# A long convolution's inverse transform: operands of its first stage exchanged, its last stage with a small table and wide products

## The chip, the cores and the metric

The kernel runs on one core of one Trainium2 chip. The time is the device time of one execution in microseconds. The core's engines work side by side: PE (matrix products; PEld is its loading of the stationary operand), ACT and DVE (elementwise work, both may read PSUM, where the PE writes), POOL (elementwise work on SBUF alone), and SP, which here only issues DMAs. SBUF and PSUM have 128 partitions. All data is 32-bit.

## The reference

One transformer-like block for 2048 tokens of 640 channels: a modulated layer norm, a gated long convolution (H3), and a modulated MLP with squared ReLU.

```python
kv_f = rfft(pad(conv4(k, shift_k) * v, S)); kf_f = rfft(pad(ssm_k, S))
y = irfft(kv_f * kf_f)[:S] + kv * ssm_D
x = q + ga * (h1(q) * y)                   # h1, h2: layer norms, scaled and shifted
out = x + gb * (relu(h2(x) @ w1 + b1) ** 2 @ w2 + b2)
```

The modulation rows (`ga`, `gb` and so on) come from `silu(c) @ w_mod`. The convolution runs per channel with transforms of length 4096.

## The kernel before, in words

**Convolution.** The 640 channels are taken as five blocks `b` of 128. A transform of 4096 is written as matrix products in two steps. A token is 64 n + i, with n from 0 to 31 and i from 0 to 63. `unit_a` (L374) contracts n with the table `cw`: four 64*64 tiles of the PE array per group of channels, copied by ACT from PSUM to `AX`. `spectrum` (L395) contracts i with twiddle tables `gb`, once for the kernel `h` and once for the data `x`; `front` (L421) multiplies the two spectra on DVE and adds on POOL, which gives `w` (in parts of `WE` and `WX`), with frequencies on partitions and 128 channels free.

**Inverse.** `back` (L449) does the first stage: the table `gi` is stationary, the products `w` move, and the result has (real or imaginary, i) on 128 partitions; ACT copies it into `QT`, per group of four channels (32 residues m, 4 channels). `unit_t` (L537) transposes four such groups on the PE and ACT copies them to `TS`, two buffers in `WX2`. `unit_y` (L548) does the last stage for one `unit_t`: the transposed data is stationary, the table `ca` (256 columns) moves, 64 columns at a time; 16 matmuls per unit, eight units per block, so 128 a block. Two units share a PSUM tile with the tag Y (two buffers). The result has token mod 128 on partitions and goes to `UP` (16 rows of 128 tokens, 128 channels) by ACT for blocks 0 to 2, by DVE for block 3; for block 4 DVE multiplies it right there with the gate. In block 4 `unit_t2` (L525) transposes half tiles instead, and the last product is cut in two (`y_rest`, L575).

**Around it.** `kv_k`, `kv_s`, `kv_v`, `kv_m` (L232 to L284) make the convolution's input for a later block: PE transposes of k (`kt`, in PSUM under tags X, T or Y), an ACT copy, three DVE passes, a DVE product with v, and a store to `kv_d`, from where `load_x` fetches it. `stats1` (L299) takes mean and variance of q's rows (`q_big`, `q_load`, L926 to L934, load them); `load_xp` (L485) loads q's columns of one block; `prep_a`, `prep_m`, `prep_p` and `gate` normalise, scale and gate; `finish_near` and `finish_add` add q. The parts of the first 256 tokens stay in SBUF, the others go through `x1_d`.

**Order.** The order on each engine is the order in which the program is written: for each block ten steps FS(b, j) (`front` and `back`) and 18 steps GS(b, s), eleven for the last block. `UNITS` (L1111) gives, by block, the steps s at which the next block's `unit_a` (first list), the `unit_t` (second) and the `unit_y` (third) are issued; `at(...)` places everything else, before or after the `unit_a` of a step (`AFTER`). In one step `unit_y` comes first, then `unit_t`. `keep_order` holds the engines to it. All loads and most stores are issued on SP, in order; `sp_dma` lets an issue wait until the one four before it has landed.

**MLP.** After the last block, eight chunks of 256 tokens go through the two products (`mlp_front` L723, `mlp_back` L805) and out by `mlp_out` (L840).

Of the kernel before, what the change touches and what calls it, by code (L numbers as in the profile page):

```python
# [11 lines left out]
F32 = mybir.dt.float32  # L12
# [6 lines left out]
P = 128  # L19
# [12 lines left out]
def _constants():  # L32
# [35 lines left out]
    ca = np.zeros((32, 2, 2, 2, 2, 2, 16, 2))  # L68
    t2 = np.arange(16)
    for h in range(2):  # L70
        nn = 2 * t2 + h
        th = 2 * np.pi * ((m[:, None] * nn[None, :]) % 64) / 64
        a, b = 2 * np.cos(th) / N, -2 * np.sin(th) / N
        a[0] = 1.0 / N
        b[0] = (-1.0) ** nn / N
        for g in range(2):
            for d in range(2):
                ca[:, g, d, 0, h, g, :, d] = a
                ca[:, g, d, 1, h, g, :, d] = b
# [6 lines left out]
        "ca": ca.reshape(128, 256).astype(f),  # L86
# [6 lines left out]
def ssm_mlp_kernel(  # L93
# [70 lines left out]
    TS = [WX[2][:, 4 * j : 4 * j + 4] for j in range(2)]  # L164
# [7 lines left out]
    ca = WX[1][:, 8:10].rearrange("p r (h n) -> p r h n", h=2)  # L172
# [26 lines left out]
    xsrc = kv_d.rearrange("(g a) (n i) -> (a n) g i", a=4, i=64)  # L199
    pt = {}  # L200
# [173 lines left out]
    def unit_a(b, i, q):  # L374
# [74 lines left out]
    def back(b, j):  # L449
        if j == 0:  # L450
            QT[b] = sb.tile([P, DG, 32, 4], F32, tag="S4", name=f"q_{b}")
# [7 lines left out]
        for u in range(4):  # L459
            w = ws[b, 2 * j + u // 2]  # L460
            for r in range(2):
                for a in range(2):
                    l = slice(64 * a, 64 * a + 64)
                    pe.matmul(  # L464
                        t[a][:, u],
                        gi[l, 4 * j + u, r],
                        w[r][l, u % 2],
# [3 lines left out]
        m = 8 * j  # L471
        for g in (slice(0, 16), slice(16, 32)) if end else (slice(0, 32),):
            for a in range(2):
                copy(
                    dve if a and end else act,
                    QT[b][:, g, m + a : m + 8 : 2, :],
                    t[a].rearrange("p m (g d) -> p g m d", d=4)[:, g],
                )
# [6 lines left out]
    def load_xp(b):  # L485
        t = sb.tile([P, NL, P], F32, tag=f"XP{b % 2}", name=f"xp_{b}")
        src = q[:, b * P : (b + 1) * P].rearrange("(l p) d -> p l d", p=P)
        for l in range(0, NL, 4):
            sp_dma(t[:, l : l + 4], src[:, l : l + 4])
        XPt[b] = t  # L490
# [31 lines left out]
    ys, tss = {}, {}  # L522


    def unit_t2(b, g):  # L525
# [788 lines left out]
```

## Time and profile before

| | |
|---|---|
| three runs | 693.88, 696.73, 690.06 us (median 693.88) |
| the profiled execution | span 692.6 us from the first to the last instruction; the page gives no time around it |
| mean granted clock of the PE | 0.990 |
| PE busy | 656.1 us (95%), 8741 matmul records, 8741 weight loads |
| DVE, ACT, POOL busy | 414.1, 326.1, 255.2 us |
| last stage `y` on the PE | 45.1 us, 1280 records |
| first inverse stage `qp` | 42.4 us, 640 records |
| transposes `t` | 22.5 us, 192 records |
| MLP | from 293.2 us to the end |

A page of the profile lists busy time per engine, then groups of instructions by line and operand names (output <- inputs), and the chain of waits that ended last. Names of tiles stand without their numbers. A busy PE isn't a PE at its peak: matmuls are pipelined and their ends are modelled. "Idle before" names what ended an engine's wait; "issue" there means that nothing in the profile explains it.

### The profile page before, as it was taken

What the parts mean: (1) busy time and instruction counts of PE and PEld (TensorE: products, weight loads), DVE (VectorE), ACT (ScalarE), POOL (GpSimd) and SP (SyncE); (2) the same over time, 40 slices, a digit from 0 to 9 for tenths busy, and PEclk for the clock granted to TensorE, in tenths of its full rate; (3) what the DMA queues carried; (4) which work ended last, traced back from release to release, by engine and by line L of the source; (5) the groups of instructions that cost most, each with busy time, mean ns of one, the idle gap of its engine ahead of it and who ended that gap; (6) DMA issues with size and microseconds to landing.
All of it is one profiled execution on the core that took longest, in us unless ns stands there. A gap on an engine that the chain in (4) does not pass through costs nothing.

```text
span 692.6 us, 20344 instructions
## 1 busy us (share of the span) xinstructions
PE 656.1 (95%) x8741; PEld 608.5 (88%) x8741; DVE 414.1 (60%) x783; ACT 326.1 (47%) x688; POOL 255.2 (37%) x299
## 2 busy tenths in 40 slices
PE   6699789898999998999999999999999999999996
PEld 5689678797898897899999999999999999999996
DVE  4257656677787587668665564555645555555633
ACT  4426556767985995547424323333233233233221
POOL 1053155548978879553500301402203204003301
PEclk9999999999999999999999999999999999999999
DMA  9996889878772463456120020010010200200001
GB/s 235 256 255 188 226 240 271 238 209 206 198 237 65 136 185 106 134 145 210 26 77 0 1 77 1 7 71 1 38 39 1 76 2 1 77 1 0 39 1 39
DMA packets 110958, 74.72 MB, mean 108 GB/s; under 512 B 48658, under 2 KB 96146, under 8 KB 110868
## 3 DMA queue, kind: packets, MB, share of 16 engines
q1 hardware_dynamic: 108912, 72.87, 37.2%
q8 instruction: 69, 1.13, 0.7%
q10 hardware_dynamic: 1892, 0.54, 0.3%
q14 instruction: 21, 0.17, 0.1%
q0 software_dynamic: 64, 0.01, 0.0%
HBM read 58.98 MB, written 14.42 MB: 106 GB/s over the span
## 4 chain that ended last, share of the span: by engine, by line
PE 83%; DMA 5%; DVE 4%; ACT 4%; issue 2%; POOL 1%; SPq 0%; POOLq 0%; DVEq 0%; ACTq 0%
PE acc L823 27%; PE h L735 23%; PE pa L383 5%; PE qp L464 5%; PE x L398 4%; PE y L555 4%; PE h L398 3%; PE h L748 2%; PE t L544 2%; PE h L739 1%; DMA p<-kv_d 1%; PE xtp L700 1%; PE vt L276 1%; PE kt L239 1%; ACT q L146 1%
## 5 line engine op out<-in xcount | busy, mean ns | idle before, releaser
L823 PE MATMUL acc<-w_S,hring 128*128 128x320 f32 x960 | 156.7, 311 | 0.2 <-DVE hring L157 0.2
L735 PE MATMUL h<-xt,w_S 128*128 128x512 f32 (+1 forms) x770 | 149.6, 340 | 0.0
L823 PEld LDWEIGHTS acc<-w_S,hring 128*128 128x128 f32 x960 | 144.8, 188 | 4.8 <-DVE hring L157 0.7
L735 PEld LDWEIGHTS h<-xt,w_S 128*128 128x128 f32 x770 | 120.1, 189 | 14.1
L157 DVE TENSOR_TENSOR hring<-mtmp,hring 128x256 fp32r<-128x256 f32 x112 | 67.4, 601 | 69.9 <-ACT hring L146 69.9
L157 POOL TENSOR_TENSOR xt<-we,xt 128x256 fp32r<-128x256 f32 x35 | 27.5, 785 | 201.2 <-ACT xt L146 201.2
L154 DVE TENSOR_TENSOR mtmp<-h,mtmp 128x256 f32<-128x256 f32 (+1 forms) x99 | 41.9, 423 | 96.5 <-ACT mtmp L780 94.0
L780 ACT ACTIVATE mtmp<-h,b1t 128x256 f32<-128x256 f32 x91 | 43.2, 475 | 113.9 <-PE h L735 113.9
L146 ACT ACTIVATE hring<-mtmp 128x256 fp32r<-128x256 f32 x112 | 46.1, 411 | 73.9 <-DVE mtmp L782 63.2
L383 PE MATMUL pa<-wx,p 64*64 64x64 f32 x2560 | 49.4, 230 | 14.0 <-issue 7.9
L383 PEld LDWEIGHTS pa<-wx,p 64*64 64x64 f32 x2560 | 44.2, 143 | 19.9 <-issue 14.2
L146 ACT ACTIVATE a<-pa 128x512 f32<-128x512 f32 x80 | 43.1, 607 | 21.9 <-PE pa L383 21.7
L151 DVE TENSOR_TENSOR wx<-x,wx 128x512 f32<-128x512 f32 x64 | 40.8, 682 | 17.1 <-PE x L398 10.2
L555 PE MATMUL y<-wx,wx 128*64 128x64 f32 x1280 | 45.1, 225 | 4.1 <-ACT wx L146 2.5
L555 PEld LDWEIGHTS y<-wx,wx 128*64 128x64 f32 x1280 | 40.3, 138 | 8.9 <-ACT wx L146 4.0
L398 PE MATMUL x<-a,gb 128*64 128x128 f32 x640 | 42.7, 279 | 3.1 <-DVE wx L151 1.8
L782 DVE SCALAR_TENSOR_TENSOR mtmp<-mtmp 128x256 f32<-128x256 f32 x91 | 39.6, 435 | 3.1
L398 PEld LDWEIGHTS x<-a,gb 128*64 128x64 f32 x640 | 37.0, 140 | 4.5 <-PE h L398 2.5
L261 DVE SCALAR_TENSOR_TENSOR KV<-kt,tap,KV 128x511 f32<-128x511 f32 (+2 forms) x48 | 35.9, 748 | 7.5 <-ACT ktail L146 5.9
L154 POOL TENSOR_TENSOR wm<-wm,wm 128x640 f32<-128x640 f32 x20 | 32.1, 1604 | 15.9 <-ACT wm L341 15.5
L146 ACT ACTIVATE q<-qp 128x512 f32<-128x512 f32 (+1 forms) x40 | 21.3, 584 | 34.5 <-PE qp L464 34.3
L146 ACT ACTIVATE xt<-we 128x256 fp32r<-128x256 f32 x37 | 15.3, 415 | 43.4 <-DVE we L705 43.4
(152 smaller groups left out, 1117.8 us busy)
## 6 DMA issues: line engine op xcount, KB each, us to landing
wm<-in_w_mod_dram SPq DMA_DIRECT2D x25, 320.0 KB, 4.2
KV<-in_A_k_dram SPq DMA_DIRECT2D x20, 256.0 KB, 4.3
KV<-in_A_v_dram SPq DMA_DIRECT2D x20, 256.0 KB, 4.5
p<-in_A_ssm_k_dram SPq DMA_DIRECT2D x20, 256.0 KB, 4.9
p<-kv_d SPq DMA_DIRECT2D x20, 256.0 KB, 4.6
xp<-in_A_q_dram SPq DMA_DIRECT2D x20, 256.0 KB, 4.3
q<-in_A_q_dram SPq DMA_DIRECT2D x15, 320.0 KB, 5.0
out_dram<-x SPq DMA_DIRECT2D x14, 320.0 KB, 2.1
```

Of the source, the lines that this page charges most:

```text
L146: act.activation(o, i, AF.Copy)
L151: eng.tensor_mul(o, a, b)
L154: eng.tensor_add(o, a, b)
L157: eng.tensor_sub(o, a, b)
L261: dve.scalar_tensor_tensor(o, tk[:, : 512 - t], tap[:, b, t : t + 1], o, op0=ALU.mult, op1=ALU.add)
L383: pe.matmul(t[e][64 * r : 64 * r + 64, g].rearrange("p m d -> p (m d)"), pt[b][l, i, 8 * q + g, :], cw[l, r], start=True, stop=True,)
L398: pe.matmul(t[64 * a : 64 * a + 64, s + r], gb[:, g, r, a], AX[b][i][:, 2 * g + a], start=True, stop=True,)
L555: pe.matmul(y[64 * h : 64 * h + 64, 4 * (g % 2) + i].rearrange("p c l d -> p (c l d)"), tss[g][:, i, 64 * r : 64 * r + 64], ca[:, r, h], s ...
L735: pe.matmul(*x, start=(b == 0 and x is both), stop=(b == NB - 1 and x is both))
L780: act.activation(r, h[:, 1], AF.Identity, bias=b1t[:, f : f + 1])
L782: dve.scalar_tensor_tensor(r, r, 0.0, r, op0=ALU.max, op1=ALU.mult)
L823: pe.matmul(acc[2 * s + i], h[:, a, s * P : (s + 1) * P], w[:, y, i * 320 : (i + 1) * 320], start=(f == 0 and ti == 0), stop=(f == NF - 1 ...
```

## The change

In `back` the two operands are exchanged: the products `w` are stationary, the table `gi` moves, and channels come out on partitions. `QT` becomes [128 channels, 64 values of i, 64 of (m, real or imaginary)]. `unit_t` transposes two values of i at a time for all 128 channels, in every block; in block 4 the copies alternate between ACT and DVE. `TS` has six buffers, in `WX2`, `WX1` and `WX3`. `unit_y` takes four `unit_t` at once: the table, now 64 rows (twice) by 32 columns, is stationary, and 512 columns (four pairs, 128 channels) move; eight matmuls of eight different 64*32 tiles, into two PSUM tiles with tag Y; two units per block. A token is now 64 n + 16 c + l, with partition 32 c + n, so a partition holds 16 tokens in a row (l), and the loads of q and the stores of the output go by c, 32 partitions at a time. `unit_a` writes `AX` with the channels in their own order. The first unit of block 4 gives l from 0 to 7, so its statistics (`finish_near(4, 0)`, `stats2(0)`) are placed at GS(4, 4) and GS(4, 5), ahead of the second unit, and `y_rest` and `unit_t2` are gone.

```diff
     def unit_a(b, i, q):
...
-            c = 64 * e + 16 * q
-            o = AX[b][i][:, :, c : c + 16].rearrange("p m (g d) -> p m g d", d=2)
-            copy(act, o, t[e].rearrange("p g m d -> p m g d"))
+            o = AX[b][i][:, :, 32 * q : 32 * q + 32].rearrange("p m (g e d) -> p m g e d", e=2, d=2)
+            copy(act, o[:, :, :, e], t[e].rearrange("p g m d -> p m g d"))
...
     def back(b, j):
...
                     pe.matmul(
                         t[a][:, u],
+                        w[r][l, u % 2],
                         gi[l, 4 * j + u, r],
-                        w[r][l, u % 2],
...
+        for a in range(2):
+            c = 16 * j + 8 * a
+            copy(
+                dve if a and end else act,
+                QT[b][:, :, c : c + 8],
+                t[a].rearrange("p u (r n) -> p n (u r)", r=2),
+            )
...
     def load_xp(b):
...
-        for l in range(0, NL, 4):
-            sp_dma(t[:, l : l + 4], src[:, l : l + 4])
+        for a in range(4):
+            sp_dma(t[32 * a : 32 * a + 32], qsrc[a, :, :, b * P : (b + 1) * P])
...
     def unit_t(b, g):
         t = ps.tile([P, 4, P], F32, tag="T", name=f"t_{b}_{g}", bufs=2)
+        n = 16 * (g % 4) + 8 * (g // 4)
         for i in range(4):
-            pe.transpose(t[:, i], QT[b][:, 4 * g + i].rearrange("p m d -> p (m d)"), ident)
-        tss[g] = TS[g % 2]
-        copy(act, tss[g], t)
+            x = QT[b][:, n + 2 * i : n + 2 * i + 2].rearrange("p n k -> p (n k)")
+            pe.transpose(t[:, i], x, ident)
+        tss[g] = TS[g % 6]
+        copy(dve if b == NB - 1 and g % 2 else act, tss[g], t)

     def unit_y(b, g):
...
+        y = [ps.tile([P, 4, P], F32, tag="Y", name=f"y_{b}_{g}_{i}", bufs=2) for i in range(2)]
+        for a in range(4):
+            for i in range(2):
+                l = slice(64 * i, 64 * i + 64)
+                pe.matmul(
+                    y[i][32 * a : 32 * a + 32].rearrange("p l d -> p (l d)"),
+                    ca[l],
+                    tss[4 * g + a][l].rearrange("p i d -> p (i d)"),
+                    start=True,
+                    stop=True,
+                )
+        for i in range(2):
+            uo = UPt[b][:, 8 * g : 8 * g + 8].rearrange("p (l i) d -> p i l d", i=2)[:, i]
             if b < NB - 1:
-                copy(act if b < 3 else dve, uo, y)
+                copy(act if b < 3 else dve, uo, y[i])
             else:
...
+                dve.tensor_mul(uo, y[i], uo)
...
     def mlp_out(n):
...
             if n < NC - 1:
                 add(dve if s else pool, X1t[n][:, s], t, X1t[n][:, s])
-                sp_dma(out[l * P : (l + 1) * P, :], X1t[n][:, s])
                 continue
             for i in range(2):
...
-                (act.dma_start if i else sp_dma)(out[l * P : (l + 1) * P, o], X1t[n][:, s, o])
+                if s or i:
+                    o = o if s else slice(0, D)
+                    for a in range(4):
+                        (act.dma_start if a % 2 else sp_dma)(
+                            osrc[a, :, 2 * n + s, o], X1t[n][32 * a : 32 * a + 32, s, o]
+                        )
+        if n < NC - 1:
+            for a in range(4):
+                sp_dma(osrc[a, :, 2 * n : 2 * n + 2], X1t[n][32 * a : 32 * a + 32])
...
     def q_load(t, l0, n):
+        for a in range(4):
+            sp_dma(t[32 * a : 32 * a + 32, 0:n], qsrc[a, :, l0 : l0 + n])
         for i in range(n):
-            sp_dma(t[:, i], q[(l0 + i) * P : (l0 + i + 1) * P, :])
             qt[l0 + i] = t[:, i]
...
-        ([0, 1, 4, 11, 13, 16, 16], [1, 3, 3, 5, 5, 6, 7, 9], [3, 4, 4, 6, 7, 8, 8, 11]),
-        ([2, 2, 5, 5, 10, 10, 12], [1, 4, 4, 7, 8, 11, 13, 14], [4, 7, 7, 11, 13, 13, 16, 17]),
-        ([1, 2, 5, 7, 8, 11, 14], [1, 2, 5, 7, 9, 11, 13, 15], [4, 7, 8, 9, 13, 14, 16, 17]),
-        ([0, 3, 4, 6, 9, 11, 14], [1, 2, 4, 7, 8, 11, 14, 14], [4, 6, 8, 10, 11, 14, 17, 17]),
-        ([], [1, 1, 2, 2, 5, 5, 6, 6], [4, 5, 5, 6, 6, 8, 9, 9]),
+        ([0, 1, 4, 11, 13, 16, 16], [1, 3, 3, 5, 5, 6, 7, 9], [6, 11]),
+        ([2, 2, 5, 5, 10, 10, 12], [1, 4, 4, 7, 8, 11, 13, 14], [9, 16]),
+        ([1, 2, 5, 7, 8, 11, 14], [1, 2, 5, 7, 9, 11, 13, 15], [9, 17]),
+        ([0, 3, 4, 6, 9, 11, 14], [1, 2, 4, 7, 8, 11, 14, 14], [9, 17]),
+        ([], [1, 1, 1, 2, 2, 3, 3, 4], [3, 6]),
```

More of the change, by code (lines that the diff above doesn't have):

```diff
@@ L1144, in ssm_mlp_kernel @@
         for s in range(11 if last else 18):
[L1145 removed]
+            if s == sy[0] and not last:
                 u_tile(b)
[L1147 removed]
+            for g in range(2):
                 if sy[g] == s:
```

94 lines of the change are left out of this document (17 added, 77 removed).

## The prediction

> **What bounds the kernel now.** I read the table of stages first: the span cut where one block of 128 channels passes from its spectral half to the half that holds the inverse's last steps. "GS" below is that second half. A row gives the stretch, its length, and each engine's busy time (with instructions), then clock, DMA share and rate.
>
> ```profile
> core 0: us, PE busy (x) PEld busy (x) DVE busy (x) ACT busy (x) POOL busy (x), PEclk, DMA share, GB/s
> 60.00:91.00 31.00, 24.50 (x712) 21.99 (x710) 19.68 (x42) 17.72 (x34) 3.91 (x12) 1.00 0.78 218
> 91.00:117.00 26.00, 25.46 (x463) 23.89 (x462) 18.15 (x32) 14.48 (x27) 16.27 (x25) 1.00 0.94 263
> 117.00:147.40 30.40, 27.75 (x776) 24.34 (x778) 19.57 (x40) 23.17 (x44) 13.15 (x18) 0.94 0.81 223
> 173.40:201.50 28.10, 26.91 (x844) 24.24 (x843) 21.62 (x31) 26.77 (x57) 22.98 (x25) 1.00 0.71 201
> 226.30:249.60 23.30, 22.41 (x752) 20.14 (x752) 14.18 (x18) 22.64 (x50) 18.33 (x13) 1.00 0.59 150
> 275.30:293.20 17.90, 17.41 (x350) 14.91 (x351) 11.79 (x26) 8.98 (x20) 10.33 (x12) 1.00 0.47 138
> 293.20:692.60 399.40, 393.77 (x2569) 370.63 (x2567) 220.46 (x461) 138.90 (x313) 88.20 (x85) 1.00 0.12 40
> ```
>
> The MLP, 399.4 us, has the PE busy for 393.8; the change touches only its stores. The rows of GS(0) to GS(3) differ: in GS(0) the PE idles 6.5 us, beside DMA at 0.78 and more; in GS(1) it has 27.75 of 30.4; in GS(2) and GS(3) the ACT is as full as the PE (26.77 of 28.1, 22.64 of 23.3). The part that changes most is `y`; the same table for its instructions alone shows what there is to win:
>
> ```profile
> 117.00:147.40 30.40, 8.48 (x256) 7.88 (x256) 0.00 (x0) 1.87 (x3) 0.94 0.81 223
> 173.40:201.50 28.10, 8.78 (x256) 7.95 (x256) 0.00 (x0) 1.98 (x3) 1.00 0.71 201
> ```
>
> **The last stage on the PE.** The timeline gives start, length and form (rows*columns of the stationary tile, then the moving operand):
>
> ```profile
> 49.03 2.06 PE L464 MATMUL qp<-wx,gi 64*128 64x128 f32 x32
> ...
> 61.69 1.16 PE L383 MATMUL pa<-wx,p 64*64 64x64 f32 x64
> 62.78 1.15 PE L555 MATMUL y<-wx,wx 128*64 128x64 f32 x32
> ```
>
> Each matmul leaves two records. `pa` uses four 64*64 tiles of the array, `y` two of 128*64: 64 records by four and 32 by two are both 16 rounds, and both take 1.09 us to the next start. So tiles run side by side, and a round of 64 columns costs 68 ns. `qp`, 16 rounds of 128 columns in 1.99 us, gives 124 ns, so each further column costs 0.88 ns and a round of 512 about 462 ns. The new unit has 16 records on eight 64*32 tiles: two rounds, **0.93 us**, against 4 x 1.09 = 4.34 us for the four units it replaces. No row shows 64*32. The bounds are one tile at a time, 16 rounds or 7.4 us, and eight; I take eight, since two and four both paid in full. At four it would be 1.85, at two 3.7. A block falls from 8.7 to 1.9 us: 6.8 us off the PE. The first inverse stage keeps its 16 matmuls of 128 columns per call, so I price the exchange of operands at zero; both waited for the POOL's product anyway.
>
> **What takes the gain's place.** In GS(2) the ACT decides:
>
> ```profile
> 186.53 0.64 ACT L146 ACTIVATE up<-y 128x512 f32<-128x512 f32 x1 [0.80 <-POOL xp L154]
> ...
> 201.77 0.64 ACT L146 ACTIVATE up<-y 128x512 f32<-128x512 f32 x1 [0.21 <-PE y L555]
> 202.64 0.60 ACT L146 ACTIVATE wx<-h 128x512 f32<-128x512 f32 x1 [0.24 <-PE h L398]
> ```
>
> These are most of its gaps in 28 us. The ACT keeps 16 forward copies, 8 transposed copies and 4 output copies per block. By form they read:
>
> ```profile
> L146 ACT ACTIVATE a<-pa 128x512 f32<-128x512 f32 x80 | 43.1, 607 | 21.9 <-PE pa L383 21.7
> L146 ACT ACTIVATE up<-y 128x512 f32<-128x512 f32 x12 | 7.6, 636 | 2.4 <-PE y L555 1.6 <-POOL xp L154 0.8
> ```
>
> `a` now gets the two-element runs that `up` had, and `up` whole runs of 128: I charge 29 ns x 16 = 0.5 us per block to the ACT and credit 0.1.
>
> Second, a new wait. A `y` unit takes both PSUM buffers of tag Y at once; the transposes `kt` of the convolution use the same two in turn. Already now:
>
> ```profile
>   DVE KV L261: 1.3, 2
> ```
>
> that is, `y` sat 1.3 us, in two places, until the DVE had finished with a `kt`. With the new order of buffers the second half of `unit_y(1,0)` follows `kt` of `kv_k(3,2)`, that of `unit_y(2,0)` follows `kv_k(4,2)`, each the PE instruction just before it, and must wait for the ACT copy and three DVE passes:
>
> ```profile
> 130.09 0.60 PE L239 MATMUL kt<-ident,KV 128*128 128x128 f32 x4
> 130.94 0.69 ACT L241 ACTIVATE KV<-kt,tap 128x509 f32<-128x509 f32 x1
> 132.03 2.32 DVE L261 SCALAR_TENSOR_TENSOR KV<-kt,tap,KV 128x511 f32<-128x511 f32 x3
> ...
> 188.95 0.66 PE L239 MATMUL kt<-ident,KV 128*128 128x128 f32 x4
> 190.02 0.69 ACT L241 ACTIVATE KV<-kt,tap 128x509 f32<-128x509 f32 x1
> 191.12 2.32 DVE L261 SCALAR_TENSOR_TENSOR KV<-kt,tap,KV 128x511 f32<-128x511 f32 x3
> ```
>
> From the end of `kt` to that of the last pass: 134.35 - 130.69 = 3.7 us in GS(1), 193.44 - 189.61 = 3.8 in GS(2). Everything on the PE behind it waits: the next forward units, transposes and `kt`. `unit_y(0,1)` meets `kv_k(2,1)` in the same way in GS(0). In GS(1) three units of 1.09 us that stood ahead of that `kt` are gone, but it also needs a K load that stands on SP behind four `p` loads (below), so I let it start at 129.5. Then y starts 3.7 us after that `kt`'s end, at 133.8, ends at 134.7, and what follows on the PE is 8.7 us of work: three forward units at 1.09, six groups of transposes at 0.55 or so, a row product of 1.3 and the second y of 0.93: 143.4 against 147.4. An instruction stall sits in this stage now:
>
> ```profile
> 135.19 0.45 PE L383 MATMUL pa<-wx,p 64*64 64x64 f32 x13 [2.61 <-issue]
> ...
> 138.54 1.06 PE L239 MATMUL kt<-ident,KV 128*128 128x128 f32 x4
> ```
>
> With it the end is 146.0. Between -4.0 and -1.4 I take **-1.8 in GS(1)**, near the small end, since the ACT, which all these groups wait for, has DMA waits of its own there. After that stall the four transposes took 1.06 us where 0.60 is usual, and the stage's granted clock is 0.94: 0.06 x 30.4 = 1.8 us lost. A new wait of 3.7 us can do that again; once in two, **+1.0**. The Trainium skill (TensorE: Matmul & The Clock Gate, Part 1: The HAM clock gate) says an idle window of about 3.4 us halves the PE clock; taken strictly, both new waits would pay, and the sum would be 2.6 higher than with my +1.0. The trace agrees only in part: the clock fell after 2.61 us, and GS(0) kept 1.00 through a stall as long.
>
> GS(2): the PE saves 6.8 and waits 3.8; the ACT, with 1.3 us of idle and 0.4 more work, lets 0.9 through: **-0.8**. GS(3) has no `kt`; its ACT has 0.7 of idle and 0.5 more work, but the PE can run four spectrum groups ahead into the next block: **-0.8**, between 0 and -2.5. Such a group reads:
>
> ```profile
> 92.03 1.04 PE L398 MATMUL x<-a,gb 128*64 128x128 f32 x16
> ```
>
> and the next starts 0.87 us later, so four are 3.5 us; the DVE's products free their buffers, and half of it, 1.75, is the most that I let through.
>
> **The last block.** Here `t` copies alternate between ACT and DVE, and the statistics for the first 256 tokens need only the first y unit.
>
> ```profile
> 276.15 1.75 DVE L151 TENSOR_TENSOR up<-up,g1row 128x512 f32<-128x512 f32 x1
> ...
> 278.68 0.98 DVE L154 TENSOR_TENSOR x<-xp,up 128x256 f32<-128x256 f32 x1
> ...
> 284.84 0.69 DVE L570 TENSOR_TENSOR up<-y,up 128x512 f32<-128x512 f32 x1 [2.21 <-PE y L555]
> ...
> 289.09 0.16 DVE L671 SCALAR_TENSOR_TENSOR nm<-mv,rs 128x2 f32<-128x2 f32 x1
> ...
> 289.36 0.80 DVE L1183 TENSOR_SCALAR mtmp<-x,rs,nm 128x256 f32<-128x256 f32 x2
> ```
>
> The DVE's order becomes: this product (to 277.9), copies of t1 and t3 (0.65 each with a transpose between, to 279.9), the fourth block's sums (0.98 in the row, 1.9 with what precedes it), two y products (2 x 0.69, to 283.2), copies of t5 and t7 with a transpose between (to 285.1), sums and statistics (2.1): `nm` at 287.2, 2 us earlier than 289.25. But the second unit's two products (1.4) now stand ahead of the DVE's half of the normalisation, which starts near 288.6 instead of 289.36: **-0.8**, between -3 and +0.5.
>
> **Loads and stores.**
>
> ```profile
> q<-in_A_q_dram SPq DMA_DIRECT2D x15, 320.0 KB, 5.0
> w2s<-in_B_w_dram SPq DMA_DIRECT2D x2, 160.0 KB, 3.1
> ```
>
> and, on SP's own timeline, block 2's `p` and the K load after it:
>
> ```profile
> 118.22 4.83 SPq L138 DMA_DIRECT2D p<-kv_d  x4
> ...
> 124.53 0.37 SPq L138 DMA_DIRECT2D KV<-in_A_k_dram  x1
> ```
>
> `q` becomes 24 loads in place of 16 (eight more on SP, all ahead of that `p`), each of 32 partitions, same bytes. SP keeps four in flight, so a load costs a quarter of its landing time: pairs that were 2 x 5.0 / 4 become 4 x 3.1 / 4, +0.6 us for each of two, about as much for the tile of three, +1.5 for the single one: up to 3.3 us of queue ahead of block 2's `p`, under the 0.94 row. The PE's forward units hide most; **+0.5**, to +3.
>
> The tail:
>
> ```profile
> 687.15 1.93 POOL L154 TENSOR_TENSOR x<-mtmp,x 128x320 f32<-128x320 f32 x2 [2.33 <-DVE mtmp L838]
> ...
> 688.04 0.81 SPq L138 DMA_DIRECT2D out_dram<-x  x2
> ...
> 689.11 0.84 ACTq L853 DMA_DIRECT2D out_dram<-x  x2
> ```
>
> Now two stores go out on ACT after the POOL's second sum (689.08). After the change six do, 0.42 us each: the last issue ends at 689.1 + 2.5 = 691.6, not 689.95. SP's fifth and sixth wait for its first two to land, about as late. **+1.6**.
>
> **Sum.** -1.8 + 1.0 - 0.8 - 0.8 - 0.8 + 0.5 + 1.6 = -1.1 on the profiled span of 692.6: 691.5. The runs' median, 693.88, is 1.3 above that span: **692.8**. A measurement of this kernel (690.06 to 696.73) tells no change from one within about 1%, 687 to 700.8.
>
> **Rivals.** *The PE's gain comes through.* If `kt` moves up with the PE, the wait shrinks or lies where it idled anyway, no instruction stall recurs and the clock holds: GS(1) gives 6.8, GS(2) and GS(3) the ACT's idle and 1.75 us of run-ahead each, 1.3 + 1.75 = 3.0 and 0.7 + 1.75 = 2.4, the last block 3: -15.2, +2.1 for loads and stores, on 693.9: 681. For it: 27.75 of 30.4. Against: the ACT's rows.
>
> *Slower: loads into 32 partitions run at a lower rate.* Between 91 and 117 us DMA carries 263 x 26 = 6.8 MB, of which seven `q` loads and one `xp` are 3.3 MB, 12.5 us. If these take 1.4 times as long, in the middle between no loss (the bytes are the same) and twice (a quarter of the partitions), block 2's `p` lands 5 us later, and the eight `q` loads of block 0, 5.0 us each by fours, add 2 x 5.0 x 0.4 = 4, of which the PE's idle 6.5 us in GS(0) covers half: 692.8 - 0.5 + 7 = 699.3, and with the stages behind `p` pushed into new waits 703. It decides once block 2's `p` comes more than 2 us late (1.15 times), since the PE has saved about that much ahead of it. The Trainium skill (SBUF — State Buffer, Door 1: The DMA port swizzle) gives 189 GB/s for 32 partitions and 328 for 128: by that the factor would be 1.7 for such a load alone. No row has a 32-partition load; the 64-partition `w2s` took 3.1 us for half the bytes, which doesn't settle it.
>
> *The change doesn't do what it says*: 64*32 tiles run one by one. Then a block costs 14.8 instead of 8.7, +6.1 in GS(1) to GS(3) and +8 on the last block's path: 720. At two tiles at a time it is a gain of 1.3 per block, and nothing shows.
>
> **Chances.** Forecast (687 to 700.8, its own range) 0.50; gain comes through 0.27; slow loads 0.16; single tiles 0.07. Faster 0.27, same 0.50, slower 0.23. The range leaves out single tiles and the far ends: 681 to 703.
>
> **What would show it.** `y` in the after profile: 160 records; a unit near 0.93 us right, 3.7 or 7.4 wrong. `y` idle before it, ended by DVE L261, near 3.7 us in GS(1) and GS(2); if it is under 1, the first rival. ACT over 95% busy in GS(2) and GS(3). `q` landing times near 3 us for pairs; above 6 for fours means the second rival. Six ACT stores behind the last sum. I'd be wrong most easily in the waits of GS(1), where PE, ACT, DVE and SP are within 3 us of each other.

## The result, and the profile after

The changed kernel takes **709.42 us** (median of five runs, 708.37 to 713.03) against 693.88 of the kernel before (five runs, 690.06 to 699.57) beside it: a ratio of 1.0263 (95% interval 1.0209 to 1.0316). The forecast was 692.8 in a range of 681 to 703. The profiled execution took 713.03 us with a span of 711.2, so the loss of 18.6 in the spans below stands for 15.5 in the medians.

The table of stages, cut at the same events as the one of before: from 60 us to the first spectrum of block 1, then by turns the spectral half and the half GS of each block, the last block's half, the MLP. The columns are stretch, length, busy time of PE, PEld, DVE, ACT and POOL, clock, DMA share, GB/s.

```profile
60.00:94.50 34.50, 22.80 (x486) 16.89 (x484) 19.69 (x42) 17.17 (x34) 3.87 (x12) 0.80 0.84 214
94.50:122.00 27.50, 25.57 (x461) 23.83 (x460) 18.15 (x32) 14.37 (x27) 16.27 (x25) 1.00 0.79 205
122.00:155.70 33.70, 25.25 (x552) 18.71 (x552) 18.74 (x38) 21.97 (x42) 13.09 (x18) 0.85 0.79 202
155.70:184.80 29.10, 25.99 (x396) 23.61 (x388) 20.65 (x31) 19.11 (x38) 20.95 (x25) 0.94 0.93 211
184.80:217.00 32.20, 25.16 (x621) 18.66 (x619) 21.78 (x34) 26.79 (x56) 22.10 (x24) 0.90 0.74 184
...
242.70:266.80 24.10, 19.60 (x526) 13.75 (x524) 13.69 (x17) 22.15 (x49) 18.60 (x14) 0.93 0.65 144
...
293.40:310.20 16.80, 14.72 (x95) 9.09 (x95) 14.66 (x29) 6.91 (x16) 10.37 (x12) 1.00 0.50 145
310.20:711.20 401.00, 393.74 (x2569) 370.55 (x2567) 220.25 (x461) 138.84 (x313) 88.06 (x85) 1.00 0.14 40
```

With the same cuts the kernel before reads 31.1, 25.8, 30.5, 26.0, 28.1, 23.1, 17.9 and 399.4 us in these rows. The losses are 3.4 in GS(0), 1.7 in the spectral half of block 1, 3.2 in GS(1), 3.1 in the spectral half of block 2, 4.1 in GS(2), 1.0 in GS(3) and 1.6 in the MLP with its tail; the last block gains 1.1. The two rows left out lose 1.6 together. In the halves with `y` the PE has less work (25.16 of 32.2 us in GS(2), before 26.91 of 28.1), and yet GS(0) to GS(3) all got longer, at a granted clock of 0.80 to 0.93, where before only GS(1), at 0.94, stood below 1.00.

The last stage itself does what it was meant to do. From the timeline, one unit at full clock, and the PE's next instruction:

```profile
69.54 0.63 PE L532 MATMUL y<-wx,wx 64*32 64x512 f32 x4
69.56 0.63 PE L532 MATMUL y<-wx 64*32 64x512 f32 x4
69.99 0.61 PE L532 MATMUL y<-wx,wx 64*32 64x512 f32 x4
70.02 0.61 PE L532 MATMUL y<-wx 64*32 64x512 f32 x4
70.56 1.09 PE L523 MATMUL t<-ident,q 128*128 128x128 f32 x8
```

That is 16 records on eight tiles in 1.02 us. But in three places the unit waits for a `kt` buffer. From the timeline, in each place the DVE's passes over `kt` and the `y` behind them, with the wait in brackets:

```profile
83.26 2.32 DVE L258 SCALAR_TENSOR_TENSOR KV<-kt,tap,KV 128x511 f32<-128x511 f32 x3
...
85.72 1.95 PE L532 MATMUL y<-wx,wx 64*32 64x512 f32 x14 [4.66 <-DVE KV L258]
...
140.53 2.32 DVE L258 SCALAR_TENSOR_TENSOR KV<-kt,tap,KV 128x511 f32<-128x511 f32 x3
...
142.99 1.07 PE L532 MATMUL y<-wx,wx 64*32 64x512 f32 x3 [3.77 <-DVE KV L258]
...
200.91 2.31 DVE L258 SCALAR_TENSOR_TENSOR KV<-kt,tap,KV 128x511 f32<-128x511 f32 x3
...
203.37 0.89 PE L532 MATMUL y<-wx,wx 64*32 64x512 f32 x3 [2.96 <-DVE KV L258]
```

11.4 us of waiting in all, in GS(0), GS(1) and GS(2); before it was 1.3. The PE's other large waits, from the list of waits between 60 and 300 us (total, times, longest):

```profile
PE t L523 <- ACT wx L141: 6.1, 4, 5.0
PE pa L380 <- DMA p<-kv_d: 3.9, 1, 3.9
```

The first stands in GS(0): the ACT there waits 5.0 us for the store of a `kv_d` tile to land (before 2.99), and the transposes wait for the ACT. From the timelines, the kernel before first:

```profile
73.59 0.69 ACT L241 ACTIVATE KV<-kt,tap 128x512 f32<-128x512 f32 x1 [2.99 <-DMA kv_d<-KV]
```

```profile
74.36 0.69 ACT L238 ACTIVATE KV<-kt,tap 128x512 f32<-128x512 f32 x1 [5.00 <-DMA kv_d<-KV]
```

The copy starts within 0.8 us of the same time in both. Before, the PE still had `y` units to work on up to there; now it is done early and idles. The second wait is block 2's `p` in GS(1). And the loads of q, KB each and median us to landing:

```profile
xp<-in_A_q_dram SPq DMA_DIRECT2D x20, 256.0 KB, 5.3
q<-in_A_q_dram SPq DMA_DIRECT2D x8, 320.0 KB, 6.3
q<-in_A_q_dram SPq DMA_DIRECT2D x8, 160.0 KB, 3.7
```

`xp` was 4.3 and a 320 KB `q` 5.0.

Two accounts offered themselves: waits of `y` for its buffers, with a halved clock behind each, or late loads. The runs below test each. All ratios are to the kernel before in the same set of runs, with 95% intervals.

### The profile page after: what moved, and what is told of

Read it like the earlier page. It is cut to its first block, busy times and chain, and to the rows that moved or that the text cites. A ratio compares the mean times of both kernels' runs of the same rounds, so it can differ in the third digit from the quotient of the medians.

```text
span 711.2 us, 18076 instructions
## 1 busy us (share of the span) xinstructions
PE 647.9 (91%) x7589; PEld 583.0 (82%) x7589; DVE 417.2 (59%) x785; ACT 325.3 (46%) x683; POOL 253.0 (36%) x299
## 4 chain that ended last, share of the span: by engine, by line
PE 61%; ACT 4%; DVE 2%; DMA 2%; issue 1%; POOL 1%; DVEq 0%; POOLq 0%; ACTq 0%
PE acc L790 26%; PE h L702 22%; PE h L715 2%; PE x L394 1%; PE h L394 1%; ACT KV L493 1%; PE h L706 1%; PE qp L460 1%; PE y L532 1%; PE xtp L667 1%; DMA xp<-in_A_q_dram 1%; ACT wx L141 1%; PE gr L935 1%; PE t L523 1%; DVE w_S L152 1%
## 5 line engine op out<-in xcount | busy, mean ns | idle before, releaser
L702 PEld LDWEIGHTS h<-xt,w_S 128*128 128x128 f32 x770 | 120.1, 189 | 14.1
L380 PEld LDWEIGHTS pa<-wx,p 64*64 64x64 f32 x2560 | 48.6, 154 | 23.8 <-issue 16.5
L380 PE MATMUL pa<-wx,p 64*64 64x64 f32 x2560 | 54.1, 242 | 13.6 <-DMA p<-kv_d 6.3
L141 ACT ACTIVATE a<-pa 128x512 f32<-128x512 f32 x80 | 45.2, 633 | 22.7 <-PE pa L380 22.3
L394 PE MATMUL x<-a,gb 128*64 128x128 f32 x640 | 44.9, 287 | 5.0 <-DVE wx L146 2.3
L394 PEld LDWEIGHTS x<-a,gb 128*64 128x64 f32 x640 | 38.9, 145 | 6.6 <-PE h L394 3.0
L394 PE MATMUL h<-a,gb 128*64 128x128 f32 x512 | 35.9, 284 | 2.7 <-ACT wx L141 2.7
L523 PE MATMUL t<-ident,q 128*128 128x128 f32 x160 | 25.6, 294 | 13.1 <-ACT wx L141 6.8
L394 PEld LDWEIGHTS h<-a,gb 128*64 128x64 f32 x512 | 30.2, 143 | 7.6 <-issue 3.8
L141 ACT ACTIVATE q<-qp 128x512 f32<-128x512 f32 x39 | 21.1, 593 | 32.9 <-PE qp L460 32.9
```

The costliest lines, as they stand in the source:

```text
L141: act.activation(o, i, AF.Copy)
L380: pe.matmul(t[e][64 * r : 64 * r + 64, g].rearrange("p m d -> p (m d)"), pt[b][l, i, 8 * q + g, :], cw[l, r], start=True, stop=True,)
L394: pe.matmul(t[64 * a : 64 * a + 64, s + r], gb[:, g, r, a], AX[b][i][:, 2 * g + a], start=True, stop=True,)
L523: pe.transpose(t[:, i], x, ident)
L702: pe.matmul(*x, start=(b == 0 and x is both), stop=(b == NB - 1 and x is both))
```

## Experiments

### Later y units

```diff
-  block 0: y at [6, 11]   block 1: y at [9, 16]   block 2: y at [9, 17]
+  block 0: y at [6, 13]   block 1: y at [11, 16]  block 2: y at [11, 17]
```

> The changed kernel with three of the ten y units issued two steps later (second unit of block 0, first units of blocks 1 and 2), so that each stands well behind the kt whose PSUM buffer its second half takes over. Theory 'waits' (the 15.5 us come from y waiting for that buffer, 11.4 us in three places, and from the halved clock behind each wait, 17 us of half clock or 8.5 us of work): the three waits go, part of it reappears as waits for loads in GS(0), so 697 to 701. Rival 'loads' (32-partition loads are late and everything behind them waits in any case): the waits move to other instructions, 706 to 709.

Measured: 703.68 us, 1.0166 (1.0093 to 1.0239), a repair of 1.0%, 6.7 us; the expected 697 to 701 was too good, and by its ratio the run lies just under the rival's 706 to 709. A difference of two such ratios is known to about 0.9%, here and below. The wait of `y` fell from 11.4 to 3.5 us, and others came up. From the list of waits:

```profile
PE t L523 <- ACT wx L141: 8.0, 5, 6.1
PE pa L380 <- DMA p<-kv_d: 6.1, 1, 6.1
PE y L532 <- DVE KV L258: 3.5, 2, 2.1
PE pa L380 <- DVE s L293: 2.9, 1, 2.9
```

Block 2's `p` is now waited for 6.1 us in place of 3.9, and the statistics (`s`, over a q tile) 2.9. So the first account holds for part of the loss, and behind it stands the second.

### The loads alone, from both sides

In the changed kernel the old loads, and in the kernel before the new ones:

```diff
-    for a in range(4): sp_dma(t[32*a : 32*a+32, 0:n], qsrc[a, :, l0 : l0+n])
+    for i in range(n): sp_dma(t[:, i], q[(l0+i)*P : (l0+i+1)*P, :])
```

with `load_xp` changed likewise; the opposite edit in the kernel before.

> The changed kernel with the loads of q as they were before (128 partitions each, 16 loads of a row of tokens and 4 per block for the columns); the tokens in them are not those that the new layout wants, so the output is not the reference's; all work is kept. Theory 'waits': q loads land in 5.0 us again, the first stage ends up to 3 us earlier, the waits of y stay at 3 to 4.7 us: 705 to 709. Rival 'loads': the 15.5 us go with them, 695 to 699.

> The kernel before with only the loads of q changed to those of the changed kernel (32 partitions each, 24 and 4 per block); the tokens in them are not those that the old layout wants, so the output is not the reference's; all work is kept. Theory 'waits': 694 to 697. Rival 'loads': 700 to 706.

Measured: the changed kernel with old loads 704.36 us, 1.0178 (1.0116 to 1.0241); the kernel before with new loads 701.79, 1.0148 (1.0090 to 1.0206). So the loads cost 0.85% in the one and 1.5% in the other, 6 to 10 us. The second of these is clear of the noise by itself; the first barely is. In the kernel before that is the second account's number; in the changed kernel it lies between the two, at the edge of the first. In the changed kernel the loads land sooner at 128 partitions (DMA issues, changed kernel with old loads):

```profile
xp<-in_A_q_dram SPq DMA_DIRECT2D x20, 256.0 KB, 4.4
q<-in_A_q_dram SPq DMA_DIRECT2D x15, 320.0 KB, 4.3
```

4.3 against 6.3 us for the same bytes, a factor of 1.47; for `xp` 1.2. In the kernel before the difference is smaller: 5.0 us with its own loads, 5.2 with the new ones of 320 KB (1.04), and 4.3 and 5.3 for `xp`. Counted as the prediction does, at a quarter of each load's median landing time, the 16 old loads of q's rows take 19.8 us of the queue in the kernel before; the 24 new ones take 24.6 there and 29.3 in the changed kernel. By this count their number weighs as well as the time of one. In the changed kernel with old loads no `pa` waits for `p` by 0.9 us or more between 60 and 300 us, and block 1's second half (from its last `qp` to the first spectrum of x of block 2) lasts 29.9 us where the changed kernel has 35.1 and the kernel before 31.9, while `y` still waits 12.4 us in all, 4.2 of them in this half. In the kernel before, whose PE waits there for no `p`, the new loads bring the wait in; from its timeline:

```profile
131.82 1.17 PE L384 MATMUL pa<-wx,p 64*64 64x64 f32 x64 [2.96 <-DMA p<-kv_d]
```

The Trainium skill (SBUF — State Buffer, Door 1: The DMA port swizzle) gives 328 GB/s for 128 partitions and 189 for 32, a factor of 1.7; the runs show 1.04 to 1.47 by landing time, with four loads under way at once.

### Both repairs

Late units, and loads and output stores of 128 partitions as before. This is the first run's edit, the old loads, and `sp_dma(out[l*P : (l+1)*P, :], X1t[n][:, s])` for the stores.

> The changed kernel with late y units, and with all its q loads, column loads and output stores as before (128 partitions, rows of tokens in the old order, so that tokens are mixed up and the output is not the reference's; all work is kept). Late units alone gave a ratio of 1.0166, old loads alone 1.0178, both against 1.0263 for the changed kernel. Theory 'two causes that add', with the tail's 1.6 us: 1.005 to 1.010, 695 to 699 us; a gain over the kernel before would need more than that, since GS(0) to GS(3) are held by ACT, DVE and DMA. Rival 'the gain on the PE comes through once both are repaired': under 0.995, 690 or less. Rival 'one cause seen twice': 1.014 or more.

Measured: 694.97 us, **1.0030 (0.9997 to 1.0064)**. The causes add: 0.97% for the units, 0.85% for the loads and 0.2% for the tail make 2.0 of the 2.6%, and the kernel came out a little better than that (the 0.2% is read from the stages, not from a run of its own). The loss is accounted for. The gain is still missing: with both repaired, the changed arithmetic isn't faster than the old one, though `y` still waits 4.2 us in it.

### Two attempts to mend the loads

One transfer for all 128 partitions, in right order, with (c, n) on the DRAM side, for the statistics' loads and the stores; and 24 loads as in the change, but from POOL's queue. Both with late units.

```diff
+    sp_dma(t[:, i], qsrc[:, :, l0 + i])                  # first
+    sp_dma(osrc[:, :, 2*n + s], X1t[n][:, s])
...
+    pool.dma_start(t[32*a : 32*a+32, 0:n], qsrc[a, :, l0 : l0+n])   # second
```

> The changed kernel with both repairs, and correct tokens: the y units two steps later as in the first experiment, and the loads of q for the statistics (16) and the output stores made of 128 partitions again, by one transfer whose DRAM side runs over (c, n); the column loads stay at 32 partitions. Theory 'two causes that add': the late units gave 1.0% and the wide loads 0.85%, the tail's 1.6 us another 0.2%, so a ratio to the kernel before of 1.005 to 1.010, 695 to 698 us. Rival 'one cause seen twice' (both repairs relieve the same waits in GS(0)): 1.012 to 1.017. If it comes under 1.000, the gain on the PE was there all along behind the two.

> The changed kernel with late y units, correct, and its 24 loads of q for the statistics issued on POOL's queue in place of SP's, so that they no longer stand ahead of the K loads and stores and of p in SP's order. If the queue order carries the cost of the loads: 693 to 699 us (ratio to before 1.000 to 1.008). If the cost is the rate at which 32 partitions are written, wherever it is issued: 702 to 706, as with late units alone. POOL's products in the first stage wait for the issues, which could cost up to 3 us in either case.

Measured: the first 738.82 us, 1.0665 (1.0605 to 1.0724), a miss by more than 40 us. In the MLP, where nothing else moves data, the chain of waits names two of its stores, and the table of stages shows the DMA engines in two such stretches:

```profile
386.41 9.89 DMA out_dram<-x
...
436.56 9.82 DMA out_dram<-x
```

```profile
386.50:396.30 9.80, 9.80 (x63) 9.15 (x62) 4.41 (x11) 2.67 (x6) 0.00 (x0) 1.00 0.22 67
436.60:446.30 9.70, 9.70 (x62) 9.07 (x61) 4.31 (x11) 2.67 (x6) 0.00 (x0) 1.00 0.24 69
```

A store of 320 KB landed in a median of 2.1 us before. Here two take 9.8 us with 0.22 to 0.24 of the 16 DMA engines busy, about four of them, and the outermost dimension of the transfer has four entries. The Trainium skill says just this (DMA: Bandwidth & Descriptors, Rules for kernel authors): an outermost dimension of fewer than 16 confines the transfer to at most that many engines; the shares of 0.22 and 0.24 agree. In the first stages the same loads cost some 25 us.

The second took 712.58 us, 1.0270 (1.0207 to 1.0333), worse by 1% than the late units alone. Its 320 KB loads landed in 7.3 us and the 160 KB ones in 8.7. POOL's queue is no way around; that the order on SP carries the cost isn't shown by it.

### Holding the clock

The three waiting `y` units get PE work that is thrown away: the first half's own matmuls nine times over; products of 128*128 by 512; or PE transposes.

```diff
+    if (b, g) in ((0, 1), (1, 0), (2, 0)):
+        for _ in range(8):
+            pe.matmul(y[0], ident, tss[4*g], start=True, stop=True)
+            # or: for i in range(4): pe.transpose(y[0][:, i], tss[4*g][:, i], ident)
```

> The changed kernel with the waits left in place, but in the same three y units the first half's four matmuls are issued nine times over (the same result written again), so that the PE is busy while it waits for the second buffer. Theory 'the clock doubles the price of a wait': the half-clock stretches behind these waits (6.8 + 6.8 + 3.4 us) are gone, 8.5 us of work come back less about 1.5 us by which the repeats overrun: 702. Rival 'the clock is a by-product' (what follows the waits is held by ACT and DMA in any case): 708 to 711, with the clock held or not.

> The changed kernel with the waits left in place; in the same three y units as in the filler experiment eight products of 128 rows by 128 columns by 512 go into the first half's buffer ahead of its own matmuls (which overwrite them), about 3.7 us of full-array work. Theory 'the granted clock follows how much of the array works, not whether the PE is busy' (the half-array filler lost it): the clock stays at 1.0 in the windows that hold the filler and the half-clock time between 60 and 300 us falls from 41 to under 30 us, time 702 to 707. Rival 'the filler itself is the cost' (the wait is not longer than the filler, so it only delays): 712 to 716, half-clock time as in the changed kernel.

> The same with the eight products replaced by 32 PE transposes of 128x128 of the same length, about 3.5 us. Theory 'transposes do not hold the clock': half-clock windows behind the three fillers as long as in the changed kernel or longer, 711 to 716. Rival 'any full-array work holds it': same as with products, within 1.5 us.

Measured: 714.40 (1.0342, 1.0263 to 1.0420), 713.79 (1.0308, 1.0263 to 1.0353) and 708.60 (1.0230, 1.0185 to 1.0275). The table of stages from 60 to 300 us for the changed kernel, the products and the transposes, in this order:

```profile
60.00:300.00 240.00, 198.34 (x3902) 164.65 (x3900) 160.00 (x252) 157.03 (x313) 142.96 (x167) 0.91 0.71 176
```

```profile
60.00:300.00 240.00, 211.07 (x3951) 170.50 (x3950) 160.93 (x254) 156.20 (x314) 144.51 (x168) 0.94 0.70 177
```

```profile
60.00:300.00 240.00, 205.30 (x4008) 171.53 (x4007) 163.00 (x260) 155.54 (x313) 147.68 (x174) 0.94 0.72 182
```

The clock rose from 0.91 to 0.94 with both, and the half-clock stretches behind the three waits are gone. The time did not follow as expected. From the start of a unit to its end the changed kernel takes 8.3, 6.8 and 6.1 us in the three places. With the repeats it was 8.6, 8.8 and 14.1, with the products 8.9, 8.1 and 8.1 (each takes two rounds of 512 columns, not one as I had reckoned), so part of their gain was lost again. With the transposes it was 7.6, 5.9 and 5.2, shorter than without, and the time moved by 0.3%, within the intervals. So of the 8.5 us that I had put on the clock behind these waits, no gain shows. That what follows them is held by ACT, DVE and DMA in any case is the likely reason; no run shows it. Nor do these runs hold the whole clock: the changed kernel spends 41 us between 60 and 300 us at half clock, 17 of them behind the three waits, and with the products or the transposes 27 us of half clock were left, all of it elsewhere or ahead of them.

The half-array repeats also show that busy isn't enough: in block 2 the clock halved in their midst. From that kernel's timeline:

```profile
201.05 0.59 PE L536 MATMUL y<-wx,wx 64*32 64x512 f32 x2
...
202.89 1.07 PE L536 MATMUL y<-wx,wx 64*32 64x512 f32 x2
```

while in blocks 0 and 1 the same repeats held it. What differs there I can't say.

### What PE time is worth

The kernel before, with less PE work in `y`, everything else unchanged. First four matmuls of 128*128 by 64 per unit for sixteen; then two of 128*64 by 256; then, with these, no ACT copies of the transposes from the third on.

```diff
-    for i in range(4): ... 4 x pe.matmul(y[64*h : 64*h+64, 4*(g%2)+i], tss[g][:, i, 64*r : 64*r+64], ca[:, r, h])
+    for h in range(2):                                   # second
+        pe.matmul(y[64*h : 64*h+64, 4*(g%2) : 4*(g%2)+4], tss[g][:, 0, 0:64], ca)
...
+    if g < 2: copy(act, tss[g], t)                       # third
```

> The kernel before with three quarters of y's matmuls left out: four matmuls of 128x128 by 64 per unit in place of 16 (the inverse's last step is not computed, the output is not the reference's), everything else, buffers and loads included, as before. The PE is relieved of about 6.5 us per block, as by the change (6.8), with none of its other effects. Theory 'the blocks are not bound by the PE', by the terms of the prediction: 3 to 6 us in all, 687 to 691. Rival 'PE work is worth its time': 20 to 30 us, 664 to 674.

> The kernel before with the PE time of y really taken away: two matmuls of 128x64 by 256 columns per unit in place of sixteen by 64 (the inverse's last step is not computed, the output is not the reference's; the four matmuls of 128x128 in the last such run took as long as the sixteen). About 0.25 us per unit in place of 1.09, so 6.7 us per block, as much as the change took away, with no other edit. Theory 'the blocks are not bound by the PE', by the terms of the prediction without the new waits and the loads: GS(1) -4, GS(2) and GS(3) -1 to -3 each, last block -2, so 683 to 688. Rival 'PE work is worth its time': -25 and more, 668 or less. Rival 'nothing at all, since the clock falls with the load': 691 to 695, half-clock time between 60 and 300 us over 20 us in place of 3.

> The same, and in blocks 0 to 3 six of the eight ACT copies of the transposes are left out as well (3.6 us of ACT per block; the data behind them are stale). Theory 'ACT holds GS(2) and GS(3) once the PE has room': both get shorter by 2 us or more against the run before it, 4 to 8 us in all. Rival 'another chain (DVE, DMA or the clock) holds them': within 1.5 us of it.

Measured: 696.93 us, 1.0040 (1.0002 to 1.0078); 687.94, **0.9935 (0.9910 to 0.9960)**; 685.19, 0.9896 (0.9862 to 0.9929). The first was no relief at all. From the rows of its tile `y` (minimum, median and maximum ns):

```profile
L553 PEld LDWEIGHTS y<-wx,wx x320: 186/192/338, 62.5 to 286.2; 128*128 128x128 f32 x160
L553 PE MATMUL y<-wx,wx x320: 219/275/476, 62.5 to 286.3; 128*128 128x64 f32 x160
```

A new stationary tile of 128*128 for each 64 columns takes 192 ns to load (138 for one of 128*64), and four such matmuls (eight records) took 0.96 us, nearly as long as the sixteen (1.09); that the loading is the reason is likely, not shown. The second run answers the question: a unit took 0.51 to 0.58 us, some 4.3 us less per block, 22 in all, and 4.5 us came through, **0.2 us for each us of PE time**. The rivals "25 and more" and "nothing" are both out. Part of what was taken from the PE went into the clock, whose mean between 60 and 300 us fell from 0.99 to 0.97, and part into the wait in GS(0): the thinned PE sits 3.74 us there until the same copy behind the `kv_d` store is done. In the third, ACT is relieved too, of 3.6 us per block; the tables of stages of the second and third run, for GS(3) and the spectral half behind it:

```profile
223.70:246.20 22.50, 20.54 (x542) 15.63 (x542) 15.29 (x19) 22.50 (x51) 19.21 (x14) 0.92 0.60 154
246.20:270.50 24.30, 22.33 (x372) 20.47 (x368) 20.61 (x27) 15.87 (x36) 19.30 (x22) 1.00 0.50 154
```

```profile
224.40:244.00 19.60, 18.73 (x538) 14.44 (x540) 14.86 (x18) 19.39 (x44) 17.00 (x12) 1.00 0.58 147
244.00:271.50 27.50, 23.48 (x373) 21.93 (x368) 21.83 (x28) 16.55 (x37) 22.27 (x24) 0.94 0.49 157
```

ACT was busy 22.50 of 22.50 us, and GS(3) gave 2.9 us when it was relieved: in these executions ACT decides there. The next half took 3.2 back. 14 us of ACT time were worth 2.7, as little as the PE's, and the two intervals overlap. Neither PE nor ACT alone holds these blocks.

### What is left between 1.003 and 0.9935

With both repairs the changed kernel has even less PE work than the thinned one and is 6.6 us slower. Three edits of it: `kt` of three `kv_k` on tag X, so that `y` waits for none; the ACT copies `a` in their old order; every `y` unit of blocks 0 to 3 three times over. And the first of them in the changed kernel with late units and its own loads.

```diff
-    (kv_k, 2, 1, "Y"), (kv_k, 3, 2, "Y"), (kv_k, 4, 2, "Y")
+    (kv_k, 2, 1, "X"), (kv_k, 3, 2, "X"), (kv_k, 4, 2, "X")
...
-    for a in range(4):
+    for a in [a for _ in range(3) for a in range(4)]:    # y thrice
```

> The kernel with late y units and the old loads and stores (tokens mixed up, output not the reference's, ratio 1.003), in which the transposes kt of kv_k(2,1), (3,2) and (4,2) take a PSUM buffer of the tag X (four buffers) in place of Y, so that y can wait for none of them. If the waits of y that were left (4.2 us in three places) and what they bring are what still holds it above the thinned kernel (0.9935): 0.994 to 0.998, 688 to 691 us. If not: 1.000 to 1.006.

> The same kernel of ratio 1.003, with the ACT copies of the forward stage in their old order of channels (607 ns in place of 633; channels come out in another order than the loads of x expect, the output is not the reference's either way). If the 26 ns x 80 copies, 2.1 us of ACT, are paid: 1.000, 2 us less. If they are hidden: 1.003 as it was.

> The kernel of ratio 1.003 (late y units, old loads and stores; output not the reference's), in which every y unit of blocks 0 to 3 is issued three times over (the same eight tiles, the same result written again): 1.9 us more of full-array work per unit, 3.7 per block, 15 us in all, about what the PE then has in the kernel before less 3. If the load on the array is what holds the clock and the unexplained 6.6 us are the halved clock's: half-clock time between 60 and 300 us falls from 37 us to under 20, and the time stays or falls, 0.996 to 1.003. If PE time is paid once the other causes are gone: 1.015 to 1.025. If both hold in part: 1.004 to 1.014, with less half-clock time.

> The changed kernel, correct, with late y units and kt on tag X as in the first run here: the best that can be had without other loads. Late units alone gave 1.0166. If the left waits are paid in full: 1.008 to 1.012, 698 to 701 us; if the loads hold it in any case: 1.015 to 1.018.

Measured: 1.0038 (1.0012 to 1.0064); 1.0045 (1.0015 to 1.0076); 1.0138 (1.0102 to 1.0174); and 706.28 us, 1.0207 (1.0172 to 1.0241), no better than late units alone. The first two answer no: neither the waits that were left nor the 26 ns per copy is the missing part; taking the waits away only changes who waits (in the changed kernel with its own loads, `pa` for `p`):

```profile
PE pa L380 <- DMA p<-kv_d: 10.2, 2, 7.2
PE t L523 <- ACT wx L141: 8.6, 4, 7.3
```

The third put 15 us on the PE and cost 1.1%, 7.5 us; the clock between 60 and 300 us rose only from 0.92 to 0.95. So added PE time is paid by half, removed PE time is returned by a fifth, and more load bought no time on balance.

The traces say where part of the 6.6 us lies. In the kernel with both repairs, GS(1), the spectral half of block 2 (cut here at its first spectrum of x) and GS(2) read:

```profile
117.70:143.70 26.00, 22.46 (x568) 16.78 (x570) 19.31 (x41) 21.87 (x42) 13.12 (x18) 1.00 0.90 249
143.70:171.80 28.10, 25.15 (x382) 22.70 (x382) 19.99 (x28) 18.87 (x39) 21.08 (x25) 0.94 0.83 207
171.80:204.10 32.30, 25.95 (x634) 19.29 (x636) 21.30 (x34) 27.78 (x58) 23.71 (x25) 0.89 0.74 194
```

With the same cuts the kernel before has 31.9, 25.2 and 28.9 us. So in GS(1) the gain did come through, 5.9 us, and it was lost again in the next two stretches. In the middle one a pass of the DVE stands in the chain, `nm` over 128x16 elements; ACT waits for it, and the PE for ACT:

```profile
150.09 3.09 DVE L302 SCALAR_TENSOR_TENSOR nm<-st,rs 128x16 f32<-128x16 f32 x1
...
153.21 1.65 ACT L494 ACTIVATE KV<-xp,nm,rs 128x128 f32<-128x128 f32 x4 [3.45 <-DVE nm L302]
...
155.40 1.26 PE L394 MATMUL h<-a,gb 128*64 128x128 f32 x16 [2.17 <-ACT wx L141]
```

The same pass takes 0.28 us in the thinned kernels and 0.34 with `y` thrice. In the twelve traces of the changed arithmetic in which it is long (2.8 to 3.1 us), the spectral half of block 2 lasts 28.1 to 29.3 us from the first spectrum to the last `qp`; with `y` thrice it lasts 23.9, in the thinned kernels 24.0 to 26.0, in the kernel before, where the pass takes 2.6, 26.0. So some 3 of the 6.6 us lie in this half, and the length of this pass is the plainest difference there. No run changed it alone, and what lengthens GS(2) stays open.

## Why the prediction was wrong

**The last stage on the PE: right.** 160 records, 1.02 us per unit at full clock (forecast 0.93); eight tiles run side by side. The rival of single tiles is out.

Two steps failed: the balance of gain and wait, and the price of the loads.

**What takes the gain's place: the mechanism right, the balance wrong.** The waits came where they were named and near their size: 3.77 us in GS(1) for 3.7, 2.96 in GS(2) for 3.8. But the sum set 6.8 us of PE gain against each of them ("the PE saves 6.8 and waits 3.8"), as if both counted the same. They don't: the thinned kernel shows that 22 us less of PE time bring 4.5, about 0.9 per block, while the late units show that 7.9 us less of waiting bring 6.7, though known only to some 6 us. With old loads on both sides they bring more (1.0178 to 1.0030, of which 0.2% is the tail's). Nor is a wait's price fixed: the last 4 us of it, taken away with `kt` on tag X, brought nothing. A wait stops everything behind it in order, the `kt` of the next piece included; a shorter instruction can leave the PE idle sooner, as in GS(0), where the `kv_d` store sets the time. GS(2) was forecast at -0.8 and came at +4.1; with old loads and its wait left it still stands at +2.4.

**GS(0) was named and left out of the sum.** "`unit_y(0,1)` meets `kv_k(2,1)` in the same way" was the longest of the three, 4.66 us, and the stage lost 3.4. The spectral halves had no term either: block 1's lost 1.7, and with old loads it lost nothing; block 2's lost 3.1, and at least 2.2 of that stayed in every repair.

**Loads: +0.5 was mis-sized, and this is the other step that failed; they cost 6 to 10 us.** I reckoned their landing from the bytes; the landing of 320 KB was 6.3 us where 128 partitions gave 4.3 to 5.1, and by my own way of counting the queue got not 3.3 us longer but 9.5 (29.3 for 19.8). "The PE's forward units hide most" failed with it: in GS(1) they waited 3.9 us for `p`, so the `kt` that I had put 12.5 us into the half came after 15.6. GS(1) was forecast at -1.8 and came at +3.2; with the old loads and its `y` wait of 4.2 us in place it came 2.0 under the kernel before. There the balance was near enough, and the loads were what failed. The second rival had this right, mechanism and price: block 2's `p` late, 699 to 703 us, and its sign, fours landing above 6 us, is there with 6.3; its factor of 1.4 lies inside the 1.04 to 1.47 measured. The kernel before with only these loads took 701.79. I gave it 0.16, and didn't think of it and the waits together: the range's upper end was that of one rival at a time.

**Clock: +1.0, mis-sized as a cause, right as a sign.** The mean between 60 and 300 us fell from 0.99 to 0.91, far more than "once in two". Behind all three waits the clock halved, in stretches of 3.4 and 6.8 us, and in five other places as well, 24 of 41 us. The Trainium skill's rule that the prediction weighed names an idle window of about 3.4 us, behind which the clock halves (TensorE: Matmul & The Clock Gate, Part 1: The HAM clock gate). The trace agrees in the main: the clock fell with waits of 4.66 and 3.77 us, but also with one of 2.96. Holding it behind these three waits moved the time by 0.3%, within the noise, so taking the rule strictly would have been right about the clock and, as far as these runs go, of little use for the time.

**GS(3), `a` copies, last block, tail.** GS(3) lost 1.0 where -0.8 was forecast; it has no `y` wait, and the chain of waits runs there through a column load of q, 7.46 us. The copies took 633 ns for 607, and undoing that changed nothing. ACT was to be over 95% busy in GS(2) and GS(3) and was at 83 and 92%. The last block gained 1.1 for 0.8, the MLP with its tail lost 1.6 for 1.6, with six stores on ACT behind the last sums; from the changed kernel's timeline:

```profile
704.13 1.92 POOL L149 TENSOR_TENSOR x<-mtmp,x 128x320 f32<-128x320 f32 x2 [2.34 <-DVE mtmp L805]
...
706.08 2.98 ACTq L821 DMA_DIRECT2D out_dram<-x  x6
```

The sum made again with measured prices: -4.5 for the PE time, 11.4 x 6.7 / 7.9 = +9.7 for the waits, +6 to +10 for the loads, +1.6 for the tail: +13 to +17, against 15.5 measured. It closes for the change as a whole, with prices that are each known to some 6 us only, so the closing proves little; for the kernel with both repairs it would give -0.9, and that one stands at +2.

## What to carry to other kernels

Before counting what an engine saves, ask what one microsecond of it is worth in that stage: where several chains run close together it may be a fifth, while a new wait in an in-order queue can cost most of its length, so don't set one against the other at par. When a change regroups work into larger units, look first at what each larger unit now has to hold at once (here two PSUM buffers shared with another producer), and move its place in the order with it. A layout that is better for the arithmetic is also a layout for its loads and stores: price them by their number, their partitions and their outermost dimension, not by bytes alone.

## What had not been expected of the hardware

The transfer with four entries outermost kept about a quarter of the DMA engines busy (0.22 to 0.24, and 9.8 us for two 320 KB stores that took 2.1 each). In `y`, a stationary tile of 128*128 took 192 ns to load, against 106 for one of 64*32 and 138 for 128*64. PE transposes held the clock as well as products did (0.94 each). The pass `nm` on DVE took 2.6 to 3.1 us in the kernel before, the changed one and most of its variants, but 0.28 to 0.34 in five others that issue the same instruction. In all 18 traces it ends within 0.05 us of the end of an instruction on POOL, which is at work all the while; where it is long, that is a product `wm`, several instructions after the one under way at its start. That points at the two engines holding each other up; it was seen and not tested.
